# Conv bands made on TensorE, theta weights by plain loads, double weight loads, two-bank PSUM tiles and an order rule for additions in a fused convolution and mixing kernel

## The chip, the cores and the metric

The kernel runs on one core of one Trainium2 chip. The metric is the device time of one execution in microseconds (us). Each kernel below was timed in several rounds on the same chip as the kernel before. A ratio is the mean time of one kernel's runs over the mean of the other's runs of the same rounds; it is therefore not quite the ratio of the medians that are quoted. Its interval is a 95% interval.

Beside the timed runs each kernel has one profiled execution. Times within an execution ("at 1021 us") come from that one.

Names: the profile calls the engines PE (TensorE, the matmuls), PEld (its weight loads), DVE (VectorE), ACT (ScalarE), POOL (GpSimd) and SP (SyncE); a "q" behind a name is the engine's queue. PSUM is the memory that the matmuls of this kernel write; its tiles are of one bank or of two, as the code calls them (512 F32 columns each). A tile "in rotation" is written again only when the engine that reads it has done so.

## The reference, cut to what matters

```
# B, S, D = 8, 4224, 192 ; 8 heads of 24 channels, 7 taps
w   = softmax(weight, axis=taps)                # the 1e-9 in the denominator is left out here
x   = causal convolution of the input along S, one row of taps per head
theta = x @ w_theta                             # 192 x 192
zr, zi = x * cos(theta), x * sin(theta)
y   = w_tok_r @ zr + w_tok_i @ zi               # two 4224 x 4224 mixing matrices, over S
u   = x + y
out = u + max(u @ w_ch, 0)                      # 192 x 192
```

## The kernel before

Tokens are cut into 33 chunks of 128. For each chunk the convolution is done on TensorE with banded matrices (`bands`), theta is a small matmul, and the sines and products give the chunk's `z` tiles. The first 11 chunks are made in the start-up, the others while TensorE mixes. The mixing matmuls (`y <- z, wt`) run in 58 steps. A step usually has two row blocks of the mixing matrices and 11 chunks, with seven products for eight by combining weights. Partial sums go to DRAM (`part`) and come back (`pv`); the last 17 steps ("final" steps) also need `x`, which is added by accumulating DMAs from `xs` in DRAM.

The PSUM tiles of everything but the mixing are four tiles of one bank each, used in turn:

```python
mmpool = ctx.enter_context(
    tc.tile_pool(name="mmps", bufs=4, space=bass.MemoryType.PSUM))
...
def bank(name, dtype=F32):
    return mmpool.tile([P, PC if dtype == F32 else 2 * PC], dtype,
                       name=name, tag="mm")
```

The bands are built on VectorE from seven masks that GpSimd makes, and the theta weights are cast by GpSimd's DMA:

```python
for k in range(KS):                        # KS = 7
    nc.vector.tensor_tensor(out=btmp[:, 1 if k else 0], in0=taps..., in1=wbf..., op=ALU.mult)
    if k:
        nc.vector.tensor_tensor(out=btmp[:, 0], in0=btmp[:, 0], in1=btmp[:, 1], op=ALU.add)
...
make_identity(nc, ident)
wth = channel_weights(moe_w_theta, "wth")  # four casting loads on GpSimd
load_chunk(1)
```

The mixing weights are loaded by row block and by quarter of the chunk's tokens, also cast by GpSimd's DMA:

```python
def load_w(self, name):                    # name "11", "21", "22", "12": row block, matrix
    ...
    st = wpool.tile([P, NQ, NW * Q], F16, name="st", tag="st", bufs=4)
    for a in range(NQ):
        nc.gpsimd.dma_start(out=st[a * Q : (a + 1) * Q, :, 0:n],
                            in_=w[tb * P : (tb + 1) * P, t0 : t0 + n]...)
```

The additions of x have no order beyond their data. The last five of the 17 final steps ("late") have theirs added into the partial sums in DRAM, four steps ahead; the twelve before them have theirs added into the tile on the chip, one step ahead:

```python
def add_x(self, i):
    if self.late:
        to = part[(self.t // NU - 1) % 2][self.tbs[i], :, :]
    else:
        to = self.pv[i]
    for cols in (slice(0, HN), slice(HN, N)) if self.late else (slice(0, N),):
        nc.gpsimd.dma_start(out=to[:, cols], in_=xs[rows, cols], accum_op=ALU.add)
```

In the start-up loop, matmuls on zeros ("warm-ups", tile `spare`) fill the places where no mixing matmul is ready yet:

```python
def between(n):
    left = more(n)          # up to n mixing matmuls
    if i < 3:
        idle(left)          # warm-up matmuls for the rest
```

## Time and profile before

| quantity | before |
|---|---|
| median of the first timed runs (range of 3) | 1478.14 us (1477.16 to 1481.53) |
| span of the profiled execution (1481.5 us, the slowest of the three) | 1479.8 us |
| TensorE busy | 1435.6 us, 97% |
| start of mixing matmul no. 220 (end of start-up) | 107.8 us |
| matmuls 5236 to 5600 (about 983 to 1071 us, "the stall") | 88.0 us |

From the page of the kernel before: the engine table (busy time, share of the span, instructions), one row of the 40 slices, the chain that ended last, some groups (line, engine, operation, output<-input, shape, count | busy us, mean ns of one | idle before, main releaser) and one group of DMA issues (KB each, median us from issue to landing).

```profile
PE 1435.6 (97%) x10083; PEld 902.6 (61%) x10083; DVE 980.7 (66%) x1120; ACT 385.9 (26%) x664; POOL 604.5 (41%) x1096
...
PE   6899999999999999999999999998799999999997
...
PE 84%; DMA 9%; POOL 4%; DVE 2%; issue 1%; ACT 0%; SPq 0%; DVEq 0%; POOLq 0%; ACTq 0%
...
L394 PE MATMUL y<-z,wt 128*128 128x384 f16 x7656 | 1312.1, 327 | 24.7 <-DVE pv L359 19.7
...
L289 POOL DMA_DIRECT2D st<-in_moe_w_tok_r_dram x448 | 244.2, 566 | 355.0 <-DVE wt L301 302.9
...
L197 ACT ACTIVATE z<-pc 128x384 f16<-128x384 f32 x132 | 58.4, 504 | 384.2 <-PE pc L190 384.0
...
L226 ACT ACTIVATE z<-v,half_pi 128x384 f16<-128x384 f32 x132 | 77.7, 589 | 32.3 <-PE v L135 31.2
...
pv<-xs POOLq DMA_DIRECT2D x24, 768.0 KB, 6.8
```

The reader is to see that TensorE is nearly always busy and is 84% of the chain that ended last, with holes only in the first slices, in slices 28 and 29 of 40 (about 1000 to 1070 us) and in the last. The mean duration of a mixing matmul is 327 ns here, but undisturbed ones start 0.162 us apart: the recorded durations overlap. So counting matmuls, not busy time, is what locates the lost time.

In the start-up, GpSimd's queue shows when loads are issued (timeline of the kernel before, GpSimd, 6.7 to 24.3 us; start, duration, what, count):

```profile
6.68 0.59 POOL L121 DMA_DIRECT2D wth<-in_moe_w_theta_dram  x1
...
8.86 2.35 POOL L177 DMA_DIRECT2D xw<-in_x_dram  x4
...
19.75 4.69 POOL L177 DMA_DIRECT2D xw<-in_x_dram  x8
```

The second chunk of x goes out at 8.9 us, the third at 19.8 us. The first conv matmul starts at 12.22 us.

In the stall, TensorE waits for VectorE, which waits for additions of x. First TensorE's waits between 980 and 1075 us (total, times, longest), then the stretch 1010 to 1055 us (length, busy us and count of TensorE, weight loads, VectorE, ScalarE, GpSimd, granted clock, DMA share, GB/s), then two VectorE instructions:

```profile
PE y L394 <- DVE pv L359: 13.2, 4, 6.0
```

```profile
1010.00:1055.00 45.00, 31.79 (x220) 19.20 (x219) 27.73 (x31) 12.44 (x26) 16.63 (x28) 0.92 1.09 290
```

```profile
1044.42 0.96 DVE L359 TENSOR_TENSOR pv<-y,pv 128x768 f32<-128x768 f32 x1 [8.92 <-DMA st<-in_moe_w_tok_i_dram]
1052.46 0.96 DVE L359 TENSOR_TENSOR pv<-y,pv 128x768 f32<-128x768 f32 x1 [5.54 <-issue]
```

The releaser named in brackets is inferred. The DMA records show the real one: the two `pv<-xs` additions were issued at 1037.45 and 1040.92 us and landed at 1044.34 and 1052.39 us, within 0.1 us of VectorE's two starts.

### The profile page before, as it was taken

To read this page: it belongs to the slowest core of one execution; us is meant where nothing else is said; L and a number is where in the kernel's file an instruction comes from. 1 tells how busy PE (TensorE), PEld (TensorE's weight loads), DVE (VectorE), ACT (ScalarE), POOL (GpSimd) and SP (SyncE) were. 2 spreads that over 40 slices of the span, in tenths; PEclk is the share of its full clock that TensorE was granted. 3 is DMA by queue.
4 is the path that set the end of the run, shared out by engine and by line. 5 is a ranking of instruction groups with operands and counts; after the bars stand their busy time and mean duration, and the time that the engine had idled before them with its cause. 6 is when DMAs were issued, how large, how long until landed. Compare 5 with 4: busy or idle time off the path is not lost.

```text
span 1479.8 us, 25342 instructions
## 1 busy us (share of the span) xinstructions
PE 1435.6 (97%) x10083; PEld 902.6 (61%) x10083; DVE 980.7 (66%) x1120; ACT 385.9 (26%) x664; POOL 604.5 (41%) x1096
## 2 busy tenths in 40 slices
PE   6899999999999999999999999998799999999997
PEld 3565666666666666666666666665466666666665
DVE  5885645454558787775666668778476667666676
ACT  5881111111135353000000015254021212222134
POOL 9743424242444542433324254553444333333330
PEclk9999999999999999999999999999999999999999
DMA  9997757464699999887868699999999989998675
GB/s 130 216 206 148 135 99 153 93 148 94 147 226 220 237 216 256 186 195 173 200 163 208 152 199 213 216 286 293 189 233 253 226 206 224 202 218 189 142 170 158
DMA packets 241318, 281.96 MB, mean 191 GB/s; under 512 B 76336, under 2 KB 209456, under 8 KB 241200
## 3 DMA queue, kind: packets, MB, share of 16 engines
q0 software_dynamic: 173280, 111.20, 54.0%
q1 hardware_dynamic: 67920, 169.14, 32.2%
q8 instruction: 79, 1.29, 0.3%
q14 instruction: 39, 0.32, 0.1%
HBM read 245.49 MB, written 108.13 MB: 239 GB/s over the span
## 4 chain that ended last, share of the span: by engine, by line
PE 84%; DMA 9%; POOL 4%; DVE 2%; issue 1%; ACT 0%; SPq 0%; DVEq 0%; POOLq 0%; ACTq 0%
PE y L394 77%; PE v L135 4%; DMA xw<-in_x_dram 3%; DMA st<-in_moe_w_tok_r_dram 3%; PE tp L144 2%; POOL st L289 2%; DMA st<-in_moe_w_tok_i_dram 2%; PE pc L190 1%; DMA part<-xs 1%; POOL xw L177 1%; DVE pv L359 1%; DMA xw<-xw 0%; DMA part<-pv 0%; DVE z L237 0%; DVE z L231 0%
## 5 line engine op out<-in xcount | busy, mean ns | idle before, releaser
L394 PE MATMUL y<-z,wt 128*128 128x384 f16 x7656 | 1312.1, 327 | 24.7 <-DVE pv L359 19.7
L394 PEld LDWEIGHTS <-wt 128*128 128x128 f16 x7656 | 738.1, 98 | 482.7 <-issue 31.5
L359 DVE TENSOR_TENSOR pv<-y,pv 128x768 f32<-128x768 f32 x324 | 308.9, 953 | 429.5 <-PE y L394 414.5
L289 POOL DMA_DIRECT2D st<-in_moe_w_tok_r_dram x448 | 244.2, 566 | 355.0 <-DVE wt L301 302.9
L289 POOL DMA_DIRECT2D st<-in_moe_w_tok_i_dram x448 | 243.7, 562 | 349.6 <-DVE wt L301 296.4
L301 DVE STREAM_TRANSPOSE wt<-st 128x1408 f16<-128x1408 f16 (+7 forms) x224 | 326.6, 1463 | 10.9 <-DMA st<-in_moe_w_tok_r_dram 8.5
L148 ACT ACTIVATE uT<-tp 128x768 f16<-128x768 f16 x132 | 105.5, 817 | 321.8 <-PE tp L144 321.8
L313 DVE TENSOR_TENSOR wt<-wt 128x1408 f16<-128x1408 f16 (+7 forms) x216 | 173.6, 804 | 10.1 <-PE y L394 6.6
L197 ACT ACTIVATE z<-pc 128x384 f16<-128x384 f32 x132 | 58.4, 504 | 384.2 <-PE pc L190 384.0
L357 ACT ACTIVATE pv<-y 128x768 f32<-128x768 f32 x66 | 53.8, 816 | 275.2 <-PE y L394 274.7
L135 PEld LDWEIGHTS <-uT 128*128 128x128 f16 x1056 | 93.4, 98 | 34.9 <-ACT uT L148 3.8
L177 POOL DMA_DIRECT2D xw<-in_x_dram x132 | 76.7, 594 | 50.5 <-DMA st<-in_moe_w_tok_r_dram 18.1
L422 DVE SCALAR_TENSOR_TENSOR pv<-v,pv 128x384 f32<-128x384 f32 x132 | 71.4, 548 | 24.5 <-PE v L135 24.0
L226 ACT ACTIVATE z<-v,half_pi 128x384 f16<-128x384 f32 x132 | 77.7, 589 | 32.3 <-PE v L135 31.2
L237 DVE TENSOR_TENSOR z<-z 128x768 f16<-128x768 f16 x132 | 73.6, 557 | 7.3 <-DMA xs<-z 2.4
L413 ACT ACTIVATE ub<-pv 128x768 f16<-128x768 f32 x66 | 52.2, 835 | 71.8 <-DVE pv L359 71.7
L135 PE MATMUL v<-wch,uT 128*128 128x192 f16 x528 | 63.8, 246 | 2.6 <-ACT uT L148 2.6
L231 DVE TENSOR_TENSOR z<-z 128x1536 f16<-128x1536 f16 x66 | 60.0, 950 | 9.1 <-ACT z L226 9.0
L226 ACT ACTIVATE z<-v 128x384 f16<-128x384 f32 x132 | 65.5, 497 | 0.0
L135 PE MATMUL v<-wth,uT 128*128 128x192 f16 x528 | 62.5, 248 | 0.8 <-ACT z L226 0.8
L347 POOL DMA_DIRECT2D pv<-xs x24 | 22.1, 935 | 71.6 <-ACT ub L413 29.3
L190 PE MATMUL pc<-xw,bands 96*64 96x192 f16 x528 | 35.4, 254 | 4.4 <-DMA xs<-z 1.9
(45 smaller groups left out, 195.3 us busy)
## 6 DMA issues: line engine op xcount, KB each, us to landing
part<-pv SPq DMA_DIRECT2D x79, 768.0 KB, 4.1
pv<-part SPq DMA_DIRECT2D x79, 768.0 KB, 6.5
out_dram<-pv SPq DMA_DIRECT2D x66, 384.0 KB, 4.5
st<-in_moe_w_tok_r_dram POOLq DMA_DIRECT2D x280, 88.0 KB, 5.1
st<-in_moe_w_tok_i_dram POOLq DMA_DIRECT2D x280, 88.0 KB, 3.9
pv<-xs POOLq DMA_DIRECT2D x24, 768.0 KB, 6.8
xs<-z SPq DMA_DIRECT2D x132, 96.0 KB, 4.6
xw<-in_x_dram POOLq DMA_DIRECT2D x121, 96.0 KB, 4.8
```

What stands on the lines that cost most here:

```text
L135: pe(nc.tensor.matmul(v[:, b * D : (b + 1) * D], lhsT=tT[:, 3 * k + b + i, :], rhs=w[:, 2 * b + i, :], start=(i == 0), stop=(i == 1),))
L148: act(nc.scalar.activation(out=uT[:, :, :].rearrange("p k s -> p (k s)"), in_=tp[:, 0 : 6 * P], func=AT.Copy,))
L177: nc.gpsimd.dma_start(out=self.xw[lo : lo + n, h, :, :], in_=x[:, t0 : t0 + n, :].rearrange("b s d -> s b d"),)
L226: act(nc.scalar.activation(**args))
L231: dve(nc.vector.tensor_tensor(out=o, in0=xv, in1=o, op=ALU.mult))
L237: dve(nc.vector.tensor_tensor(out=z[:, o, :], in0=z[:, a, :], in1=z[:, b, :], op=ALU.subtract))
L289: nc.gpsimd.dma_start(out=st[a * Q : (a + 1) * Q, :, 0:n], in_=w[tb * P : (tb + 1) * P, t0 : t0 + n] .rearrange("(bt i) s -> i bt s", bt=NQ),)
L301: dve(nc.vector.transpose(self.w[name][:, 0 : self.n, :, :], self.st[name][:, :, 0 : self.n * Q] .rearrange("p bt (c j) -> p c bt j", j=Q),))
L313: dve(nc.vector.tensor_tensor(out=self.w[name][:, 0 : self.n, :, :], in0=self.w[a][:, 0 : self.n, :, :], in1=self.w[b][:, 0 : self.n, :, : ...
L359: dve(nc.vector.tensor_tensor(out=o, in0=yv, in1=o, op=ALU.add))
L394: pe(nc.tensor.matmul(y[cn][:, q, 0:BH], lhsT=self.w[wn][:, c, :, :].rearrange("p bt i -> p (bt i)"), rhs=chunks[k].z[:, zn, q * BH : (q + ...
L422: dve(nc.vector.scalar_tensor_tensor(out=pk, in0=channel_mix(self.uT[i, g], k, wch), scalar=0.0, in1=pk, op0=ALU.max, op1=ALU.add,))
```

## The change

Its intent: have the bands ready earlier by making them with 32 small matmuls instead of VectorE's 13 products and sums over masks; free GpSimd's queue of the four casting theta loads; halve GpSimd's weight-load issues and ScalarE's instructions for conv and sines; and tie every addition of x in GpSimd's queue behind the last weight load issued before it in the program, so that the additions are not moved ahead.

The diff, cut to its core:

```diff
-        tc.tile_pool(name="mmps", bufs=4, space=bass.MemoryType.PSUM)
+        tc.tile_pool(name="mmps", bufs=2, space=bass.MemoryType.PSUM)
...
-        return mmpool.tile([P, PC if dtype == F32 else 2 * PC], dtype,
+        return mmpool.tile([P, 2, PC if dtype == F32 else 2 * PC], dtype,
...    (conv, theta and output: one 768-wide instruction on both banks
...     in place of two 384-wide ones)
-        def load_w(self, name):
+        def load_w(self, m):
...
-            st = wpool.tile([P, NQ, NW * Q], F16, name="st", tag="st", bufs=4)
+            st = wpool.tile([P, 2, NQ, NW * Q], F16, name="st", tag="st", bufs=2)
...
-                nc.gpsimd.dma_start(
+                last["w"] = nc.gpsimd.dma_start(        # both row blocks in one load
...
-                nc.gpsimd.dma_start(
+                add = nc.gpsimd.dma_start(
                     out=to[:, cols], in_=xs[rows, cols], accum_op=ALU.add
                 )
+                tc.add_manual_dep(add.ins, last["w"].ins.name, NOSYNC, reason="order")
...
+    for rows, i, part_w in channel_pieces(moe_w_theta):
+        nc.sync.dma_start(out=stage[i // 2][rows, i % 2, :], in_=part_w)   # plain
...
+    def idle(n):
+        if n > 0:
+            spare = banks("spare")          # warm-ups now take a tile from the rotation
...
+    taps = constp.tile([KS, H], F16, name="taps")
+    nc.vector.tensor_tensor(out=taps, in0=wkT, in1=wrcp[0:KS, :], op=ALU.mult)
+    idle(12)
+    bp = banks("bp")
+    for q in range(Q):                      # Q = 32
+        pe(nc.tensor.matmul(bp[0 : 2 * WR, 0, q * H : (q + 1) * H],
+            lhsT=sel[:, Q - 1 - q : Q - 1 - q + 2 * WR], rhs=taps, start=True, stop=True))
+    nc.vector.tensor_scalar_mul(out=bands[:, :, 0, :], in0=bv, scalar1=block[:, 0:1])
+    nc.scalar.activation(out=bands[:, :, 1, :], in_=bv, func=AT.Copy, scale=block[:, 1:2])
+    for i in range(2):
+        nc.vector.tensor_copy(out=wth[:, 2 * i : 2 * i + 2, :], in_=stage[i])   # the cast
```

The masks, VectorE's band products and GpSimd's theta loads are removed. Smaller edits of the start-up come with it and are not shown, among them: the warm-ups are 384 instead of 512 wide and no longer wait for the identity matrix, and the second step's weight loads stand before the start-up loop instead of in it.

## The prediction

> **What bounds the kernel now.** TensorE: busy 1435.6 of 1479.8 us (engine table), 84% of the chain of waits. Its 7656 mixing matmuls follow each other every 0.162 us where undisturbed (stretches table, 120-850 us: 100% busy). Counting matmuls per stretch, I estimate its lost time at 39 us before 115 us (start-up), 17 us between 1010 and 1070 us, 9 us in the tail. Only there can the change win.
>
> **Start-up.** In the timeline the first conv matmul starts at 12.2 us, after the bands that VectorE builds from 6.1 us. POOL makes seven masks (1.5 us) and issues four theta loads (2.2 us), so the second x chunk is issued at 8.9 us, the first mixing weights at 11.2, the third chunk at 19.8; the third conv (24.8 us) stops for it until 26.5. After: 32 small band matmuls of about 0.07 us (12 transposes take 0.83 us) and two parallel evictions: bands near 9 us, weights and chunks issued 3 to 7 us earlier. [...]
>
> **ScalarE** is 80-90% busy at 20-100 us. Per chunk it spends 4 x 0.504 (conv) + 4 x (0.589 + 0.497) (sines) = 6.4 us; with half the instructions at 768 wide (copies of that width: 0.82 us, so 0.19 fixed) about 5.1. Against it: with two PSUM tiles instead of four TensorE may wait 0.3-0.8 us at a time. Start-up gain: 8 us (3 to 13).
>
> **Weight loads.** 896 POOL issues of 0.564 us (488 us) become half as many of about 0.6. POOL mostly waits for VectorE (599 us): not critical. But its loads use eight semaphores in turn, so each issue waits for the eighth before it to land; twice the bytes per issue loosens that. It matters at 1014-1053 us: issues go one per 2 us, loads land after 8 us (20 at worst), two adds of x (pv<-xs) go out at 1037 and 1041, VectorE waits 8.9 and 5.5 us, TensorE 6.0, 3.0 and twice 2.0 for VectorE, and its clock halves. The backlog comes from 18 DRAM adds (part<-xs, 10 us to land), hoisted to 952-1013 us although only the last steps need them. The change ties each add behind the weight loads of its place in the program: these move to about 1270-1390 us, where DMA has room. Gain: 14 us (6 to 17).
>
> **Elsewhere** nothing; loss from the two-tile rotation (chunk phases 430-570 and 880-1010 us, tail): about 1 us, at most 7.
>
> **Prediction:** 1478 - 8 - 14 + 1 = 1457 us; 8 in 10 within 1444 to 1469. Faster by over 2%: 0.20; within 2%: 0.79; slower: 0.01.
>
> **Signs that it is right:** first conv near 9 us, no wait for x chunks before 30 us; steady state from 106 instead of 115 us; part<-xs after 1250 us; no TensorE wait over 2 us and full clock around 1030 us; POOL busy near 370 us; evictions of pc and v 0.8-0.9 us; 120-1000 us unchanged in length.
>
> **What would make it wrong:** start-up limited by DMA throughput (engines 117-123% busy at 20-80 us); TensorE waiting for PSUM tiles; the second row block's weights, loaded 4.9 instead of 6.9 runs (of seven per step) before use, arriving late in the congested stage; the moved adds delaying the last steps.

What the trace of the kernel before shows of the hardware that the text names: GpSimd's 1078 DMA issues name eight semaphores in turn, and of the 1070 that have an eighth one before them none starts until 0.28 us after that one has landed; of the 26 issues between 1014 and 1054 us, 10 start within 0.30 us of that landing. TensorE's granted clock was 0.50 from 1034.4 to 1037.8 and from 1044.6 to 1048.1 us. The weight loads issued between 1010 and 1055 us landed after 11.3 us (`w_tok_r`) and 8.3 us (`w_tok_i`) in the median, the slowest after 20.2; the 18 additions `part<-xs` after 10.2 us. The DMA share between 1270 and 1390 us was 0.85, against 1.21 between 970 and 1010 us and 1.09 between 1010 and 1055 us.

## More of the kernel before

The stages are cut by counting mixing matmuls in the trace in order of start: 220 is shortly after the start-up, 5236 to 5600 surround the only large hole later on. The same counts are used for all kernels.

The runs e1 to e4, e5 to e8, and e9 and e10 were taken on three different chips (11, 10 and 7), each group beside the kernel before on its own chip; across groups, ratios are compared and not times.

## The result, and the profile after

The kernel after took 1482.97 us in the median (1481.72 to 1485.46, 4 runs), the kernel before 1478.35 us (1477.16 to 1481.53, 4 runs) in the same rounds. The ratio is 1.003, interval 1.0008 to 1.0052: the time is the same within 2%, and very slightly longer, about 4.4 us. It was predicted at 1457 us and lies outside the range of 1444 to 1469 us.

The stage table of the profiled executions shows where the predicted 21 us went. (Its span differs by less than the timed runs do; the profiled execution of the kernel before was the slowest of its runs.)

| stage (mixing matmuls) | before, us | after, us | difference | predicted |
|---|---|---|---|---|
| start-up (to no. 220) | 107.81 | 111.69 | +3.9 | -8 |
| middle (220 to 5236) | 874.89 | 875.55 | +0.7 | about 0 to +1 |
| stall (5236 to 5600) | 88.00 | 83.93 | -4.1 | -14 |
| late (5600 to 7600) | 381.05 | 381.06 | 0.0 | 0 |
| tail (7600 to the end) | 28.08 | 30.04 | +2.0 | (within the +1) |
| span | 1479.83 | 1482.26 | +2.4 | -21 |

The page of the kernel after, the lines that answer to those of before:

```profile
PE 1437.9 (97%) x10115; PEld 906.2 (61%) x10115; DVE 973.2 (66%) x1043; ACT 366.7 (25%) x468; POOL 384.5 (26%) x655
...
L288 POOL DMA_DIRECT2D st<-in_moe_w_tok_r_dram x232 | 133.2, 583 | 532.1 <-DVE wt L301 490.8
...
L197 ACT ACTIVATE z<-pc 128x768 f16<-128x768 f32 x66 | 53.7, 814 | 383.5 <-PE pc L190 383.5
...
L227 ACT ACTIVATE z<-v,half_pi 128x768 f16<-128x768 f32 x66 | 59.6, 903 | 43.2 <-PE v L135 43.2
...
pv<-xs POOLq DMA_DIRECT2D x24, 768.0 KB, 10.4
```

What the change was meant to relieve was relieved: GpSimd's busy time fell from 604.5 to 384.5 us and ScalarE's instructions from 664 to 468. Twice the width costs less than twice the time: 814 ns instead of 504 for `pc`, 805 instead of 497 for `v`, and 903 instead of 589 for `v` with `half_pi`. So ScalarE's work on a chunk's conv and sines fell from 6.4 to 5.0 us (2 x 0.814 + 2 x (0.903 + 0.805)), as predicted. None of this shortened the span.

**Start-up.** The timeline of VectorE in the kernel after, 5.8 to 14.8 us:

```profile
6.04 0.22 DVE L629 MEMSET wch<- 128x192 uint32 x1
...
8.88 0.36 DVE L563 CAST wth<-stage 128x384 f16<-128x384 f32 x1 [2.49 <-DMA stage<-in_moe_w_theta_dram]
9.77 0.36 DVE L563 CAST wth<-stage 128x384 f16<-128x384 f32 x1 [0.53 <-DMA stage<-in_moe_w_theta_dram]
...
10.80 0.15 DVE L546 TENSOR_TENSOR taps<-wkT,wrcp 7x8 f16<-7x8 f32 x1
13.76 0.48 DVE L556 TENSOR_SCALAR bands<-bp,block 96x256 f16<-96x256 f32 x1 [2.81 <-PE bp L550]
```

and of ScalarE, the other half of the bands:

```profile
14.34 0.47 ACT L559 ACTIVATE bands<-bp,block 96x256 f16<-96x256 f32 x1 [6.11 <-DVE bands L556]
```

The reader is to see the order. In the program the two casts (L563) stand after the bands. In VectorE's queue they stand in front of `wsum` and `taps`: the build doesn't keep the order of the text (the MEMSET of `wch`, a line near the end, runs at 6.04 us). VectorE then ran nothing from 6.4 to 8.9 us, though the exponentials that `wsum` and the taps need were done at 6.7 us: it stood at the first cast until the theta weights landed. The taps came at 10.80 us. (In this profile the loads landed late: VectorE's first instruction on `weight` starts at 5.84 us, in those of e2 and e4 to e8 at 4.45 to 5.03; the first cast starts at 8.88, in e4 and e5, with the same order, at 8.29 and 8.22. That part is not the order's.) The band matmuls then took 11.01 to 13.65 us and two evictions followed one after the other, and the first conv matmul started at 14.86 us instead of 12.22.

TensorE's waits in the first 115 us, first before, then after:

```profile
PE spare L580 <- POOL ident masks.py:199: 6.8, 1, 6.8
...
```

```profile
PE bp L550 <- DVE taps L546: 4.6, 1, 4.6
PE tp L144 <- ACT z L227: 4.0, 8, 1.3
PE spare L526 <- ACT z L227: 3.2, 4, 0.8
...
PE pc L190 <- ACT bands L559: 1.2, 1, 1.2
```

New are the wait for the taps, and waits of transposes (`tp`) and of warm-ups (`spare`) until ScalarE's sines have emptied a PSUM tile. With two tiles in rotation, a warm-up that computes nothing has to wait for a tile, and everything behind it in TensorE's queue waits too.

**Stall.** TensorE's waits between 980 and 1075 us, the stretch 1010 to 1055 us, and the two VectorE instructions, after:

```profile
PE y L395 <- DVE pv L360: 10.3, 3, 8.3
```

```profile
1010.00:1055.00 45.00, 34.29 (x251) 21.23 (x250) 33.22 (x38) 12.46 (x16) 9.83 (x15) 0.93 1.10 285
```

```profile
1039.26 0.96 DVE L360 TENSOR_TENSOR pv<-y,pv 128x768 f32<-128x768 f32 x1 [1.59 <-issue]
1051.35 0.96 DVE L360 TENSOR_TENSOR pv<-y,pv 128x768 f32<-128x768 f32 x1 [9.58 <-issue]
```

The DRAM additions did move away, as predicted (view of the tile `part`, GpSimd's additions, before and after: duration min, median, max in ns, first and last start):

```profile
L347 POOL DMA_DIRECT2D part<-xs x18: 797/1132/2428, 952.8 to 1118.4; - x18
```

```profile
L347 POOL DMA_DIRECT2D part<-xs x18: 905/1270/1575, 1280.8 to 1396.4; - x18
```

But the two additions `pv<-xs` that the stall waits for were issued earlier (1021.25 and 1032.13 us) and took longer to land: 17.9 and 19.1 us instead of 6.9 and 11.5. They landed at 1039.18 and 1051.27 us, the second only 1.1 us sooner than before. The DMA share of the stretch is 1.09 before and 1.10 after: no lighter. With 12 additions (`part<-xs`, issued at 952 to 1014 us before) gone, the share fell from 1.21 to 1.01 between 970 and 1010 us. From 1010 to 1055 us it did not fall: two `part<-xs` fewer were issued there, but one transfer of 768 KB more each of `pv<-part`, `part<-pv` and `pv<-xs` (6, 3 and 3 instead of 5, 2 and 2), and 12.82 MB were moved instead of 13.04. Why the two additions take so long to land is not shown. A full DMA stage is the author's reading; against its being all, in e6, with the same code there, two of them took 20.7 and 21.0 us at a share of 0.91.

**Tail.** TensorE's waits after 1436 us, before and after:

```profile
PE v L135 <- ACT uT L148: 2.6, 5, 1.0
...
```

```profile
PE v L135 <- ACT uT L148: 1.5, 3, 1.0
PE tp L144 <- DVE pv L424: 1.3, 2, 0.8
...
```

New is the wait of transposes for VectorE's 768-wide output instruction, 0.956 us, to give its two-bank tile back.

### The profile page after: what moved, and what is told of

It reads as the page before. It is cut to its first block, busy times and chain, and to the rows that moved or that the text cites. A ratio compares the mean times of both kernels' runs of the same rounds, so it can differ in the third digit from the quotient of the medians.

```text
span 1482.3 us, 24448 instructions
## 1 busy us (share of the span) xinstructions
PE 1437.9 (97%) x10115; PEld 906.2 (61%) x10115; DVE 973.2 (66%) x1043; ACT 366.7 (25%) x468; POOL 384.5 (26%) x655
## 4 chain that ended last, share of the span: by engine, by line
PE 90%; DMA 3%; DVE 3%; ACT 1%; issue 1%; POOL 1%; SPq 1%; DVEq 0%; ACTq 0%; POOLq 0%
PE y L395 81%; PE v L135 5%; PE tp L144 3%; PE pc L190 2%; DMA pv<-xs 1%; DMA xw<-in_x_dram 1%; ACT z L227 1%; DVE pv L360 1%; DVE z L232 1%; POOL st L288 1%; DMA xw<-xw 1%; DVE z L238 1%; DMA part<-pv 0%; POOL xw L177 0%; SPq L209 0%
## 5 line engine op out<-in xcount | busy, mean ns | idle before, releaser
L395 PE MATMUL y<-z,wt 128*128 128x384 f16 x7656 | 1297.0, 326 | 18.2 <-DVE pv L360 16.1
L288 POOL DMA_DIRECT2D st<-in_moe_w_tok_r_dram x232 | 133.2, 583 | 532.1 <-DVE wt L301 490.8
L288 POOL DMA_DIRECT2D st<-in_moe_w_tok_i_dram x232 | 133.1, 583 | 492.8 <-DVE wt L301 480.0
L313 DVE TENSOR_TENSOR wt<-wt 128x1408 f16<-128x1408 f16 (+7 forms) x216 | 173.5, 803 | 10.2 <-PE y L395 6.6
L197 ACT ACTIVATE z<-pc 128x768 f16<-128x768 f32 x66 | 53.7, 814 | 383.5 <-PE pc L190 383.5
L424 DVE SCALAR_TENSOR_TENSOR pv<-v,pv 128x768 f32<-128x768 f32 x66 | 62.9, 956 | 27.3 <-PE v L135 19.0
L227 ACT ACTIVATE z<-v,half_pi 128x768 f16<-128x768 f32 x66 | 59.6, 903 | 43.2 <-PE v L135 43.2
L135 PE MATMUL v<-wch,uT 128*128 128x192 f16 x528 | 54.2, 246 | 1.6 <-ACT uT L148 1.5
L135 PE MATMUL v<-wth,uT 128*128 128x192 f16 x528 | 54.3, 246 | 1.3 <-ACT z L227 1.0
L227 ACT ACTIVATE z<-v 128x768 f16<-128x768 f32 x66 | 53.1, 805 | 0.0
L144 PEld LDWEIGHTS <-z 128*128 128x128 f16 x396 | 27.9, 99 | 16.7 <-issue 9.4
```

Of the source, the lines that this page charges most:

```text
L135: pe(nc.tensor.matmul(v[:, k, b * D : (b + 1) * D], lhsT=tT[:, 3 * k + b + i, :], rhs=w[:, 2 * b + i, :], start=(i == 0), stop=(i == 1),))
L144: pe(nc.tensor.transpose(tp[:, 0, k * P : (k + 1) * P], u[:, k * P : (k + 1) * P], ident))
L227: act(nc.scalar.activation(**args))
L288: last["w"] = nc.gpsimd.dma_start(out=st[a * Q : (a + 1) * Q, 0:nb, :, 0:n] .rearrange("i r bt s -> i (r bt) s"), in_=w[self.tbs[0] * P : ...
L313: dve(nc.vector.tensor_tensor(out=self.w[name][:, 0 : self.n, :, :], in0=self.w[a][:, 0 : self.n, :, :], in1=self.w[b][:, 0 : self.n, :, : ...
L395: pe(nc.tensor.matmul(y[cn][:, q, 0:BH], lhsT=self.w[wn][:, c, :, :].rearrange("p bt i -> p (bt i)"), rhs=chunks[k].z[:, zn, q * BH : (q + ...
```

## The experiments

The theory after reading the two traces has four parts. (1) The casts ahead in VectorE's queue cost most of the start-up. (2) Two tiles in rotation, shared with the warm-ups, cost start-up and tail. (3) The order rule does help in the stall, but what remains there is two additions that land late in a stage with a DMA share of 1.10. (4) Double loads help little. The rivals: the start-up is bound by DMA; the two-bank tiles pay for themselves through ScalarE; the hole in the stall is made by weights that arrive late with double loads; bands on TensorE are no faster than on VectorE.

Ten kernels ran; all gave correct results. The kernel before had, in the rounds of e1 to e4, a median of 1478.94 us (7 runs); in those of e5 to e8, 1480.82; in those of e9 and e10, 1478.69.

| kernel | median us | ratio to before, interval | start-up | stall | tail |
|---|---|---|---|---|---|
| before | 1478.35 | 1 | 107.81 | 88.00 | 28.08 |
| after | 1482.97 | 1.003, 1.0008 to 1.0052 | 111.69 | 83.93 | 30.04 |
| e1, before with the order rule | 1474.44 | 0.9974, 0.9958 to 0.9989 | 108.42 | 80.47 | 28.73 |
| e2, after with casts last | 1477.76 | 0.9999, 0.9979 to 1.0019 | 105.58 | 82.31 | 30.04 |
| e3, before with two-bank tiles | 1482.92 | 1.0031, 1.0016 to 1.0045 | 107.15 | 89.07 | 29.85 |
| e4, after with early additions | 1472.76 | 0.9963, 0.9947 to 0.9979 | 110.53 | 73.32 | 30.03 |
| e5, after with single loads | 1479.28 | 0.9992, 0.9975 to 1.0009 | 109.19 | 81.75 | 30.04 |
| e6, e2 without warm-ups | 1476.81 | 0.9974, 0.9956 to 0.9992 | 103.51 | 86.17 | 30.04 |
| e7, four one-bank tiles, casts last, early additions | 1462.26 | 0.9881, 0.986 to 0.9902 | 102.04 | 73.68 | 28.27 |
| e8, e7 with single loads | 1465.59 | 0.9899, 0.9883 to 0.9915 | 105.66 | 73.32 | 28.29 |
| e9, e7 without warm-ups | 1458.56 | 0.9861, 0.9844 to 0.9877 | 99.47 | 73.32 | 28.27 |
| e10, e7 without the order rule | 1465.45 | 0.9909, 0.9894 to 0.9923 | 101.94 | 76.81 | 28.58 |

The stage from 5600 to 7600 was 381.05 or 381.06 us in all. The middle was 875.55 us in every kernel with two-bank tiles and 874.89 to 875.02 in every other.

### e1: the order rule alone

The edit, on the kernel before:

```diff
-                nc.gpsimd.dma_start(                       # weight load
+                last["w"] = nc.gpsimd.dma_start(
...
-                nc.gpsimd.dma_start(                       # addition of x
+                add = nc.gpsimd.dma_start(
...
+                tc.add_manual_dep(add.ins, last["w"].ins.name, NOSYNC, reason="order")
```

> The kernel before, plus only the rule that an add of x is issued behind the weight loads of its place in the program. My prediction's theory (the 18 hoisted DRAM adds clog the queue): they move after 1250 us, TensorE's lost time at 1010-1070 us falls from 17 to under 5 us, 12 to 14 us faster in all. Rival (the stage is short of DMA throughput and the adds to pv themselves come late): the stall stays, 10 us or more, and the whole run gains under 5 us.

Measured: 1474.44 us, ratio 0.9974, the stall 80.47 us instead of 88.00. The order rule is worth 7.5 us of the profiled stage and is the part of the change that pays: about half of the 14 us that the prediction gave it. TensorE still waits 7.1 us for VectorE there. In the timed runs it is worth less: 0.0026, about 4 us (2 to 6). The two profiled spans differ by 6.3 us, for the one of the kernel before was a slow execution, so 7.5 us is likely too high for a usual run. Neither expectation held whole: the gain stays under the rival's 5 us and far under the theory's 12 to 14, but the stall did shrink.

### e2: the casts behind the bands

```diff
-    nc.vector.tensor_scalar_mul(
+    half_band = nc.vector.tensor_scalar_mul(
         out=bands[:, :, 0, :], in0=bv, scalar1=block[:, 0:1]
     )
...
-        nc.vector.tensor_copy(out=wth[:, 2 * i : 2 * i + 2, :], in_=stage[i])
+        cast = nc.vector.tensor_copy(out=wth[:, 2 * i : 2 * i + 2, :], in_=stage[i])
+        tc.add_manual_dep(cast.ins, half_band.ins.name, NOSYNC, reason="order")
```

> The changed kernel, with VectorE's two casts of theta ordered behind its half of the bands. Theory (the compiler put the casts, which wait for the plain loads, ahead of the sum of the exponentials, so the bands are late): the taps come right after the exponentials, first conv near 11.5 us instead of 14.9, and the 3.4 us carry through to the end of the start-up (mixing matmul number 220 near 108.5 us instead of 111.7), run 3 us shorter. Rival (start-up is paced by DMA or by ScalarE, not by its beginning): first conv earlier, but matmul 220 within 1 us of 111.7.

VectorE's timeline in e2, from 6 to 15 us:

```profile
6.32 0.15 DVE L546 TENSOR_TENSOR taps<-wkT,wrcp 7x8 f16<-7x8 f32 x1
8.42 0.48 DVE L556 TENSOR_SCALAR bands<-bp,block 96x256 f16<-96x256 f32 x1 [1.95 <-PE bp L550]
8.82 0.63 DVE L563 CAST wth<-stage 128x384 f16<-128x384 f32 x2
```

The taps come at 6.32 us instead of 10.80, the first conv matmul starts at 9.52 us instead of 14.86 (predicted: near 9), and the start-up ends at 105.58 us instead of 111.69. The order of the queue cost 6.1 us in these two profiled executions, and 5.0 against e4, which has the start-up code of the change (110.53); the ratios, 1.003 and 0.9999, give 4.6 us. The first conv chunk came 2.7 us earlier than before, yet the start-up ended only 2.2 us earlier than before: from the first to the second chunk's conv, 7.0 us passed (9.52 to 16.56), where the kernel before needed 4.8 (12.22 to 17.02). TensorE's waits in e2's start-up still hold the two lines of the tile rotation:

```profile
PE tp L144 <- ACT z L227: 3.9, 8, 1.3
PE spare L526 <- ACT z L227: 3.2, 4, 0.8
```

### e3: two-bank tiles alone

The two-bank part of the diff on the kernel before: two tiles of two banks, 768-wide instructions, and the warm-ups' tile taken from the rotation:

```diff
-        tc.tile_pool(name="mmps", bufs=4, space=bass.MemoryType.PSUM)
+        tc.tile_pool(name="mmps", bufs=2, space=bass.MemoryType.PSUM)
...
-    spare = bank("spare")
...
     def idle(n):
+        if n > 0:
+            spare = banks("spare")
```

> The kernel before, with only the two-bank PSUM tiles (two in rotation) and the warm-up matmuls taking a tile of the rotation as in the changed kernel. If the short rotation costs the start-up: first mixing matmul 3 to 5 us later than 23.7 us though the first conv stays at 12.2; matmul 220 later than 107.8 by 2 to 4 us; tail (after the last mixing matmul) 1.5 us longer. If the lost start-up is all from the late bands: matmul 220 at 107.8 or up to 2 us earlier, for ScalarE has 1.3 us less to do per chunk. The middle stall stays at 17 us in both.

Measured: 1482.92 us, ratio 1.0031: 4.6 us longer (0.31% of 1478). The profile shows 0.7 us of it in the middle and 1.8 us in the tail. The first mixing matmul starts 2.7 us later than before (26.43 instead of 23.69 us), but the start-up ends at 107.15, 0.7 us earlier. So on the kernel before, the two-bank tiles cost nothing in the start-up. TensorE waits 6.8 us for tiles there (4.0 and 2.8 us), but the 3.4 us for which it waited for DMA before convs in the kernel before are gone: some of the new waits stand where TensorE would have waited anyway. Whether ScalarE's shorter work wins back the rest was not separated. The remainder is in the stall (1.1 us), within the noise of single profiles, and in the difference between the profiled and the timed runs. The two-bank tiles are a small loss by themselves.

### e4: the additions of the first two final steps made early, in DRAM

The first two of the twelve final steps that add x into the tile on the chip do so in the stall, at a DMA share of 1.10. The edit treats them as the late steps are treated, but 12 steps ahead, at about 730 us, where DMA has more room (a share of 0.79 between 700 and 760 us in the kernel after):

```diff
+            self.early = NSTEP - NU <= t < NSTEP - NU + 2
...
-            if self.late:
+            if self.late or self.early:
                 to = part[(self.t // NU - 1) % 2][self.tbs[i], :, :]
...
+        if t + 12 < NSTEP and steps[t + 12].early:
+            for i in range(len(steps[t + 12].tbs)):
+                found.append((3.3 + 1.7 * i, lambda i=i: steps[t + 12].add_x(i)))
```

> The changed kernel, with the adds of x for the first two final steps (four row blocks) done in DRAM twelve steps earlier, where the DMA engines have room, so that their pv tiles need one plain load only. Theory (VectorE waits for two pv adds that take 18 to 19 us to land in a stage where DMA is saturated): the waits of 1.6 and 9.6 us on VectorE and of 8.4 us on TensorE near 1040-1052 us go away, lost time at 1010-1070 us falls from 13 to 3 us or less, run 8 to 11 us shorter than the changed kernel, 1472 us. Rival (general saturation: anything that is loaded in this stage comes late): the stall moves to the plain loads or the weights and 6 us or more of it stay.

TensorE's waits between 980 and 1075 us, and the stretch 1010 to 1055 us, in e4:

```profile
PE y L396 <- DVE pv L361: 1.6, 1, 1.6
```

```profile
1010.00:1055.00 45.00, 43.01 (x314) 26.97 (x313) 39.25 (x44) 13.37 (x18) 9.15 (x16) 1.00 0.99 245
```

The waits for VectorE fell from 10.3 to 1.6 us, the granted clock was 1.00, and the stage took 73.32 us instead of 83.93. In the timed runs the ratio went from 1.003 to 0.9963, about 10 us. Together with the landings above, within 0.1 us of VectorE's two starts, this shows what the stall after the change consisted of: the additions that landed late, not the weight loads, which were the same double loads in both. (With four transfers fewer the stage also had a lower DMA share, 0.99; what that alone is worth was not separated.)

### e5: the change with single loads

```diff
-        def load_w(self, m):
+        def load_w(self, name):             # one row block per load, as before
...
-            st = wpool.tile([P, 2, NQ, NW * Q], F16, name="st", tag="st", bufs=2)
+            st = wpool.tile([P, NQ, NW * Q], F16, name="st", tag="st", bufs=4)
```

> The changed kernel with one load per matrix, quarter and row block again (four buffers instead of two double ones, the places in the program of before, the order rule kept). Theory (a double load can go out only when both transposes of the step before are done, and the adds of x to pv stand behind it): the middle stage, from mixing matmul 5236 to 5600, takes about 81 us as in the run with the order rule alone (80.5) plus 1 for the PSUM tiles, instead of 83.9. Rival (the double loads help or do nothing there): 84 us or more. Start-up (matmul 220) within 1.5 us of 111.7 in both, since what paces it is the late bands.

Measured: 1479.28 us, ratio 0.9992, against 1.003 of the change: in the timed runs the change is about 5.6 us faster with single loads, in other rounds and with intervals that just touch. The stall was 81.75 us, where three kernels with double loads and the same code there gave 83.93, 82.31 and 86.17. No effect of the double loads on the stall can be told from that scatter. The start-up ended 1.3 to 2.5 us earlier than in the two kernels that share the change's start-up code (110.53 and 111.69); whether that is the loads or scatter stays open in this setting. With four tiles (e8) the sign is the other way.

### e6: no warm-ups in the start-up loop

On e2, so with the casts last:

```diff
         def between(n):
-            left = more(n)
-            if i < 3:
-                idle(left)
+            more(n)
```

> The run with the casts last, and no warm-up matmuls once the convs have begun (the twelve at the start stay). If the warm-up matmuls, which take PSUM tiles of the short rotation and stand in TensorE's queue, lengthen the first chunks: second chunk's conv near 14 us instead of 16.6, first mixing matmul near 21 instead of 24.3, matmul 220 near 103 instead of 105.6. If the cold clock costs as much, or if DMA paces the start-up, matmul 220 stays at 105 to 107.

The start-up ended at 103.51 us instead of 105.58, and the ratio went from 0.9999 to 0.9974 (other rounds, intervals that overlap; e9 repeats the result). The warm-ups are there to keep TensorE's clock up, and in this pair they did (from 18 to 24 us the granted clock was 1.00 with them, 0.50 without; in e9, also without them, 0.80). The stretches of e2 and e6 from 10 to 24 us (the third number from the end is the granted clock):

```profile
10.00:14.00 4.00, 3.99 (x23) 1.68 (x24) 0.00 (x0) 1.62 (x2) 3.84 (x7) 0.57 1.54 149
...
18.00:24.00 6.00, 4.17 (x41) 2.77 (x39) 1.27 (x2) 4.50 (x6) 4.12 (x8) 1.00 1.45 206
```

```profile
10.00:14.00 4.00, 2.85 (x27) 2.36 (x28) 0.00 (x0) 2.31 (x4) 3.83 (x7) 0.50 1.49 161
...
18.00:24.00 6.00, 4.88 (x35) 3.67 (x35) 3.36 (x5) 4.37 (x7) 4.08 (x8) 0.50 1.32 185
```

Without the warm-ups the granted clock stayed at 0.50 for these 14 us, and the start-up was nevertheless shorter: the second chunk's conv started at 14.06 us instead of 16.56. At half the clock the time was less than double: in the kernel before, eight conv matmuls took 0.52 us at a granted clock of 1.00 (at 12.22 us) and 0.85 us at 0.50 (at 30.08 us). So a group of eight at 0.50 loses 0.33 us here, less than the 0.8 us of the longest of the warm-ups' four waits for a tile. (The column says nothing before a trace's first clock record. In the kernel after that stands at 21.4 us: the column showed 1.00 for 14 to 18 us while eight conv matmuls took 0.85 us.)

### e7: four one-bank tiles, casts last, early additions

This is the change with its PSUM tiles undone and the repairs of e2 and e4; bands on TensorE, plain theta loads, double loads and the order rule stay.

```diff
-        tc.tile_pool(name="mmps", bufs=2, space=bass.MemoryType.PSUM)
+        tc.tile_pool(name="mmps", bufs=4, space=bass.MemoryType.PSUM)
...    (conv, theta and output 384 wide again, as in the kernel before)
+    spare = bank("spare")                    # one tile for all warm-ups
...    (the edits of e2 and e4)
```

> Candidate: the changed kernel with one-bank PSUM tiles (four in rotation) as before, casts last, early adds for the first two final steps; bands on TensorE and double loads kept. From the stages measured one by one I add up: start-up 105 to 106, 120-980 us 874.9, middle stage 73.5, then 381.1, tail 28.1 to 28.7: 1463 us. If the two-bank tiles were what made the start-up of the run with casts last shorter than before (105.6 against 107.8), start-up is 107 or more.

Measured: 1462.26 us, ratio 0.9881. The repairs of e2 and e4 take 0.0031 and 0.0067 off the change's ratio of 1.003, which would give 0.9932; the one-bank tiles take the remaining 0.0051, 7.5 us, if the effects add up (each ratio is known to about 0.002, so this remainder to some 6 us). The profiled stages give 5.9 us: start-up 102.04 instead of e2's 105.58, middle 874.96 instead of 875.55, tail 28.27 instead of 30.04. The two lines of the rotation are gone from TensorE's waits before 115 us, of which the four longest are now:

```profile
PE y L394 <- DVE pv L359: 4.1, 3, 2.5
PE y L394 <- DVE z L229: 3.8, 4, 1.5
PE spare L532 <- DVE noise L509: 2.4, 1, 2.4
PE pc L188 <- ACT bands L565: 1.2, 1, 1.2
```

ScalarE's instructions are the narrow ones again, and the start-up is shorter all the same. The last line is the wait for the second band eviction (below).

### e8: e7 with single loads

The edit is that of e5, on e7.

> The same candidate without the double loads: before, plus bands on TensorE with casts last, the order rule and the early adds. If the double loads are worth nothing: within 1.5 us of the other candidate at every stage, 1463 us. If they help start-up by getting the weights out earlier: start-up 1.5 to 4 us longer here. If they cost in the middle stage: middle stage shorter here (72).

Measured: 1465.59 us. Against e7 of the same rounds that is 3.3 us more, the runs do not overlap (1465.22 to 1465.79 against 1461.49 to 1464.56), though the intervals of the two ratios do, and the stage table puts all of it in the start-up: 105.66 instead of 102.04. The wait is visible in e8's first 115 us and absent in e7's list:

```profile
PE pc L188 <- DMA xw<-in_x_dram: 3.7, 2, 2.9
```

In e8 the mixing weights take 16 issues where e7 has 8, so GpSimd issues the third chunk of x later: at 17.28 us, against 12.91 in e7. Fewer issues pay where GpSimd's queue holds up a load that TensorE needs soon, which in these runs is only here. In the stall e7 and e8 do not differ (73.68 and 73.32). Against e1, which has the order rule and everything else of the kernel before, e8's start-up is 2.8 us shorter (105.66 instead of 108.42): that is what the bands on TensorE and the plain theta loads, with the smaller start-up edits, bring with four tiles. The first conv starts at 10.37 us instead of 12.39, so the rival that bands on TensorE are no faster falls; how the 2.8 us divide was not separated.

### e9: e7 without warm-ups

The edit is that of e6, on e7.

> This is e7 (one-bank tiles, bands on TensorE, double loads, casts last, early adds; 1462.26 us) without the warm-up matmuls inside the start-up loop. Theory A: the warm-ups only delayed work because two two-bank tiles were shared between them and the recurrence; with four one-bank tiles they are harmless and keep the TensorE clock up, so mixing matmul no. 220 starts no earlier than in e7 (102.0 us), at 102 to 105, and the time is 1462 to 1465. Theory B: the warm-ups delay the start-up whatever the tiles, as in e6 against e2 (2.1 us): matmul 220 starts at 99.5 to 101 and the time is 1459 to 1461. Stall and tail stages as in e7 (73.7 and 28.3).

Measured: 1458.56 us (1457.09 to 1459.80, 4 runs), ratio 0.9861, interval 0.9844 to 0.9877. It beats both kernels and is the best that ran. Theory B held: the start-up ended 2.6 us earlier (99.47 us), although with four tiles and one tile for all the warm-ups no warm-up in the loop waits (e7's list above names `spare` only for the first one, before the loop). So sharing the tiles is not the only way in which they delay: they also occupy the queue in front of work that is ready. The first chunk's conv shows it (TensorE, e7 and then e9):

```profile
11.24 1.78 PE L532 MATMUL spare<-noise 128*128 128x384 f16 x5
12.95 0.85 PE L188 MATMUL pc<-xw,bands 96*64 96x192 f16 x8
```

```profile
10.35 1.49 PE L188 MATMUL pc<-xw,bands 96*64 96x192 f16 x16 [1.21 <-ACT bands L565]
```

In e7 five warm-ups stand in front of the second half of the conv; in e9 both halves run in one go. Which of the two ways counts for how much in e6 was not separated.

### e10: e7 without the order rule

```diff
-                tc.add_manual_dep(add.ins, last["w"].ins.name, NOSYNC, reason="order")
```

> This is e7 without the rule that orders the DRAM additions behind the last write-back; everything else is as in e7 (1462.26 us, stall stage 73.7). Theory A: the early additions carry the whole gain in the stall stage, the rule is then worth nothing: stall stage 73 to 75, time 1461 to 1464. Theory B: without the rule the additions are hoisted again to where they queue ahead of write-backs and loads, and cost what the rule took out in e1 (7.5 us): stall stage 77 to 82, time 1466 to 1471.

The text says that the rule orders the additions behind the last write-back. That is a slip: it orders them behind the last weight load. Measured: 1465.45 us, stall 76.81 us, between the two theories' ranges. The additions were indeed moved ahead again, 15 of them between 937 and 1050 us, and some that e4 had meant for about 730 us to 620 to 650 us. In the timed runs the ratio is 0.0028 higher than e7's (of other rounds, and the intervals overlap), about 4 us, and in the stage 3.1 us. So with the critical additions early the order rule keeps less than half of what the profiled stage gave it in e1 (7.5 us); by the timed runs, 0.0026 there and 0.0028 here, it keeps its worth. Which is right stays open.

## Why the prediction was wrong

Three steps failed: the bands were late because of casts that nobody had placed (1, and 2 in small), the two-tile rotation was costed too low (3), and the cause named for the stall carried about half of it at most (4). Of the 26 us between 1457 and 1483, the timed runs give 4.6 us to the first (e2), 9.9 to the third (e4) and, if the effects add up, some 7.5 to the second (what is left of e7's gain).

1. **"VectorE builds the bands from 6.1 us ... After: 32 small band matmuls of about 0.07 us and two parallel evictions: bands near 9 us." The mechanism was right, a wait in front of it was overlooked.** With nothing else changed but the place of the casts, the first conv started at 9.52 us (e2). As built, the two casts stood ahead of the taps in VectorE's queue, which put the bands at 14.8 us and the start-up at +3.9 us instead of -8. The prediction costed the theta loads' departure from GpSimd's queue. It did not ask in which queue the new casts would stand and what they wait for. e2 measures this omission at 5.0 to 6.1 us of the profiled start-up and 4.6 us of the timed runs.

2. **"Two parallel evictions" failed.** ScalarE's half started when VectorE's had ended: 13.76 to 14.24 us, then 14.34 to 14.81. In e2 it was the same: 8.42 to 8.90 us, then from 9.00. Both traces name VectorE's half as what ended ScalarE's idle time (6.11 us in the kernel after, 1.60 in e2). Both read the same bank of the same tile; whether that made the order is not shown, and splitting the two halves over two banks was not tried. The cost is about 0.5 us. The band matmuls took 2.64 us for 32, 0.083 each, a small miss (in e2 1.78 us, 0.056 each).

3. **"Against it: with two PSUM tiles instead of four TensorE may wait 0.3-0.8 us at a time. Start-up gain: 8 us" and "Elsewhere ... about 1 us" were mis-sized.** The waits for tiles add up to 4.0 and 3.2 us in the start-up. Going back to four tiles took 3.5 us off the start-up, 0.6 off the middle and 1.8 off the tail (e7 against e2), some 7.5 us in the timed runs. On the kernel before, whose bands and x chunks come later, the same tiles cost nothing in the start-up (e3). "Elsewhere" was +2.6 us instead of +1. The warm-ups, which the change moved into the rotation, were not costed at all. ScalarE's relief (6.4 to 5.0 us per chunk) was sized right, but it did not decide the start-up: e7 has the old ScalarE work and is faster. With four tiles and the casts last, the start-up gain was 5.8 us (107.81 to 102.04), inside the predicted 3 to 13. Without the warm-ups it was 8.3 us (99.47); that this meets the predicted 8 is luck, for the prediction left the warm-ups in.

4. **"The backlog comes from 18 DRAM adds ... Gain: 14 us" named a cause that carries about half at most.** Only 12 of the 18 stood there, at 952 to 1014 us; the other six ran at 1096 to 1118 us. The adds moved as predicted, to 1281 to 1396 us. Alone, that gained 7.5 us in the profiled stage and about 4 us in the timed runs (e1). What remained was the two `pv<-xs` additions themselves: issued earlier, they took 17.9 and 19.1 us to land, at a DMA share that stayed at 1.10. The prediction read "two adds of x go out at 1037 and 1041" as a consequence of the backlog ahead of them, and assumed that they would land quickly once issued earlier. Making them elsewhere (e4) brought a further 10.6 us (9.9 in the timed runs). In the kernel as changed, the profile showed only 4.1 us of gain in the stage; the rest of e1's 7.5 us is within what single profiles of the same code scatter there (82.3 to 86.2), and how it divides stays open.

5. **"Twice the bytes per issue loosens that" in the stall was not seen.** No run shows an effect of the double loads there. Their gain was in the start-up, 3.6 us (e7 against e8), and only with four tiles. In the change as built, single loads were the faster ones (e5, 5.6 us in the timed runs, of other rounds); that stays unexplained.

6. **Right:** ScalarE's durations at the new widths (0.81 us for `pc`, 0.90 and 0.81 for `v`; VectorE's output instruction, 0.96 us, was a little over the predicted 0.8 to 0.9), GpSimd's busy time (384.5 us, predicted near 370), the move of `part<-xs`, and a middle that stayed within 0.7 us. The sign "full clock around 1030 us" did not come: the granted clock of the stretch was 0.93; it was 1.00 in e4 and in e7 to e9, which have the early additions and the order rule.

Of the reasons given for a wrong prediction, "TensorE waiting for PSUM tiles" came true; "start-up limited by DMA throughput" did not decide it: e2, e7 and e9 shortened the start-up step by step at a DMA share of 1.05 to 1.54 between 10 and 30 us (e2 and e9).

## What to carry to other kernels

When a change moves work to another engine, write down that engine's queue in the order of the trace, not of the text: one instruction that waits for a load can hold up everything behind it (here VectorE ran nothing from 6.4 to 8.9 us), and an order rule between two instructions can be worth more than the work saved (the one of e2 was worth 4.6 us in the timed runs). Here, wider PSUM tiles in a smaller rotation saved instructions on the engine that empties them (ScalarE, 664 to 468) and made the engine that fills them wait (TensorE, 4.0 and 3.2 us in the start-up); count waits for tiles before counting instructions, don't let warm-up work share the rotation, and measure whether it pays at all. In a stage with much DMA (a share of 1.10), an earlier issue need not bring as much earlier a landing: the two additions went out 16.2 and 8.8 us earlier after the change and landed 5.2 and 1.1 us earlier (in e1, 13.9 and 12.9 earlier out, 7.6 and 8.6 earlier in). What removed the wait was to move the transfer to another stage.
